# RetNet attention into a routed expert layer: scores in four quarters of the array, logits every second step, second keys turned in a scores' bank, and another order of the first loads

## The chip, the cores and the metric

The kernel runs on one core of a Trainium2 chip. The metric is the device time of one execution in microseconds. Five engines work side by side from queues of their own: TensorE (PE in the profile, PEld for its weight loads), VectorE (DVE), ScalarE (ACT), GpSimd (POOL) and SyncE (SP), which here issues nearly all DMAs.

## The reference

Two layers follow each other. The first is a recurrence over 768 positions for 4 batches of 8 heads of width 64; its result is the input of a layer of 8 experts, each row of 512 going to the expert with the highest logit.

```python
gamma = 1.0 - 2.0 ** (-5.0 - np.arange(H))
for t in range(S):                      # attention: q, k, v are (4, 8, 768, 64)
    state = gamma * state + k[:, :, t] (outer) v[:, :, t]
    y[:, :, t] = scale * q[:, :, t] @ state
x = y as rows of 8 heads x 64           # (3072, 512)
logits = x @ w_gate                     # (3072, 8)
e = argmax(logits); gate = softmax(logits)[e]
out = gate * (relu(x @ w1[e]) @ w2[e])  # w1 (8, 512, 1024), w2 (8, 1024, 512)
```

All data are float32.

## The kernel before

The attention runs in `STEPS = 12` steps, numbered 0 to 11. A step takes 128 positions of a pair of batches (`b` is 0 or 1) with all 8 heads, that is four pairs of heads `a`; `j` is the head within a pair, on partitions 0 to 63 or 64 to 127. The decay is folded into q and v: `scale_q` (GpSimd, for two steps at a time) and `scale_v` (GpSimd) write `qs` and `vs`. TensorE turns keys (`turn_k`, the tile `trk`, copied to `kT` by ScalarE) and queries (`turn_q`, `trq`, copied to `qT`), both one step ahead and inside the step before. In a step TensorE then does, in this order: `scores` (k times q, the tile `sc`, 64 rows by 128 columns of the array per product), `with_state` (q times the old state into `y`), `logits` of the step before (its `parts`), the turns of the next keys, `logits_of` (two transposes of the logits), in odd steps the turns of the next queries, `next_state` (the tile `new`), and `within` (masked scores times v, also into `y`). VectorE multiplies the scores with the causal mask (`am`), turns the finished `x` into rows (`to_rows`, the tile `xg`), reduces the logits (`lg`) and adds the state. ScalarE copies `x` out of PSUM.

Routing runs in pieces between the steps: `place(i)` is a generator, and `step(s, at)` pulls its next piece at a fixed place of a step (the table `WHEN`). `place(0)` covers steps 0 to 4 and begins in step 5, `place(1)` covers steps 5 to 8 and begins in step 9, `place(2)` covers the rest. `place(1)` ends with the row numbers `src_e` that GpSimd gathers for the early part of expert 0; after these gathers GpSimd writes one element of `w1t`, and only then may SP issue the first weights. In step 10 the second half of the masks (`am[1][1]()`) stands behind the routing's pieces. Step 11 ends in `early_rows`, and then the early expert layer begins (`hp`, `layer1`).

PSUM has eight banks: the tag `sc` has four (scores, `parts`, `trq`), `tr` two (`trk`, `new`, and the routing's `rk` and `found`), `y` two. Banks of a tag are taken in turn. Every engine's order is the order written in the program (`tc.manual_schedule`).

SP issues the DMAs in program order: a first list (lines 852 to 863), and then in step s the q, k and v of step s + 3 and the store of step s - 1 (`x_d<-xg`, four DMAs). `k` and `v` have 8 buffers, `q` 4, `xg` 3.

After the attention come the expert layers, one expert after the other (`p` at lines 233, 333, 246 and 474).

Of the kernel before, what the change touches and what calls it, by code (L numbers as in the profile page):

```python
# [21 lines left out]
P = 128  # L22
# [31 lines left out]
def kernel(  # L54
# [513 lines left out]
    with ExitStack() as actx:  # L568
# [19 lines left out]
        def load(nm, s, b, parts=1):  # L588
            m, b1, e = where[s]
            src = {"q": q, "k": k, "v": v}[nm]  # L590
            if nm == "q":
                to = att.tile([P, H, 2 * D], F32, tag=nm, name=nm, bufs=4)
                for part in (ts(i, H // parts) for i in range(parts)):
                    nc.sync.dma_start(to[:, part, :], src[2 * b1 + b, part, ts(m, 2 * P), :].rearrange(
                        "h (t e) d -> t h (e d)", e=2))
            else:
                to = att.tile([P, H, D], F32, tag=nm, name=nm, bufs=8)
                nc.sync.dma_start(to, src[2 * b1 + b, :, ts(2 * m + e, P), :].rearrange("h t d -> t h d"))  # L598
            raw[nm, s, b] = to
# [9 lines left out]
        def scale_v(s, b, by=nc.gpsimd):  # L609
            vs = att.tile([P, H, D], F32, tag="vs", name="vs", bufs=4)  # L610
            by.tensor_tensor(out=vs, in0=raw.pop(("v", s, b)), op=ALU.mult,  # L611
                             in1=inner(dec[:, ts(NC + 2 * where[s][0] + where[s][2], H)], D))
            raw["vs", s, b] = vs
# [5 lines left out]
        def pairs_of(tag, bufs, name):  # L619
            return ps(tag, bufs, name).rearrange("p (a t) -> p a t", a=HP)  # L620
# [10 lines left out]

        def turn_k(s, b):
            kT = att.tile([P, HP, P], F32, tag="kT", name="kT")
            tr = pairs_of("tr", 2, "trk")
            heads_first(raw["k", s, b], tr)
            nc.scalar.copy(out=kT, in_=tr)  # L636
            front[s, b] = kT
# [4 lines left out]
        def scores(s, b):  # L642
            kT, qT = front.pop((s, b)), q_of(s, b)
            sc = [pairs_of("sc", 4, "sc") for _ in range(2)]
            am = [att.tile([P, HP, P], F32, tag=f"am{j}", name=f"am{j}") for j in range(2)]
            for a in range(HP):
                for j in range(2):
                    r = ts(j, D)
                    nc.tensor.matmul(sc[j][:, a, :], lhsT=kT[r, a, :], rhs=qT[r, a, :], start=True, stop=True)  # L649

            def mask():
                for j in range(2):
                    nc.vector.tensor_tensor(out=am[j], in0=sc[j], in1=middle(causal[:, :], HP), op=ALU.mult)  # L653

            return am, mask
# [67 lines left out]

        early, wa = [], []

        def logits(s):
            bank = ps("sc", 4, "parts")
            parts = bank[:, 0 : 2 * P]
            m = P // DT
            for dt in range(DT):  # L730
                nc.tensor.matmul(parts[ts(dt, m), :], lhsT=wg[:, dt, :], start=True, stop=True,  # L731
                                 rhs=x[s][:, dt, :, :].rearrange("p b t -> p (b t)"))
            lgT = att.tile([P, 2 * P], F32, tag="lgT", name="lgT", bufs=1)
            nc.scalar.copy(out=lgT, in_=parts)
            return lgT, bank

        def logits_of(s, lgT, bank):
            tr = bank[:, 2 * P : 4 * P].rearrange("p (b t) -> p b t", b=2)
            for b in range(2):
                nc.tensor.transpose(tr[:, b, :], lgT[:, ts(b, P)], ident)  # L740
            return lambda: nc.vector.tensor_reduce(
                lg[:, 2 * s : 2 * s + 2, :], tr.rearrange("p b (a e) -> p b e a", a=DT)[:, :, 0:E, :], axis=AX.X,
                op=ALU.add)

        MOST_T = 2 * max(b - a for a, b in zip(NEXT, NEXT[1:]))

# [101 lines left out]
        def load_all(nm, s):  # L848
            for b in range(2):
                load(nm, s, b)  # L850
# [2 lines left out]
        load("k", 0, 0)  # L853
        load("q", 0, 1)
        load("k", 0, 1)
        nc.sync.dma_start(wg[:, :, 0:E], w_gate.rearrange("(dt p) e -> p dt e", p=P))
        load_all("v", 0)
        load_all("k", 1)
        load_all("v", 1)
        load("q", 2, 0)  # L860
        load("q", 2, 1)
        load_all("k", 2)
        load_all("v", 2)
        ctx.enter_context(tc.manual_schedule(engines={PE, ACT, POOL, DVE, SP}))
        xTa = first.tile([P, DT, EARLY], F32, tag="xTa", name="xTa")
# [32 lines left out]
        def step(s, at):  # L898
            for _ in range(WHEN.get(s, "").count(at)):
                next(rest, None)  # L900

        for s in range(STEPS):
            if s + 3 < STEPS:
                if s % 2:
                    load_all("q", s + 3)
                load_all("k", s + 3)
                if s == 7:
                    store(5)
                if s + 4 < STEPS:
                    load_all("v", s + 3)  # L910
            if s % 2 and s + 1 < STEPS:
                scale_q(s + 1, 1)
            if s + 2 < STEPS:
                for b in range(2):
                    scale_v(s + 1, b)
            if s % 2 == 0 and s + 2 < STEPS:
                scale_q(s + 2, 0)
            if s in (1, 2):
                nc.gpsimd.memset(xs2[s % 2], 0.0)
            if s:  # L920
                am = [scores(s, b) for b in range(2)]
                am[0][1]()
                step(s, "m")
                if s + 2 != STEPS:
                    am[1][1]()
            y = outputs()
            if s + 1 == STEPS:
                logit = logits(s - 1)
                rows_in_order()
            if where[s][0] or where[s][2]:  # L930
                with_state(s, y)

            def ahead():
                for b in range(2):
                    turn_k(s + 1, b)

            def ahead_q():
                if s % 2:
                    for b in range(2):
                        turn_q(s + 1, b)  # L940

            if s:
                if s + 1 < STEPS:
                    logit = logits(s - 1)
                    ahead()
                reduce = logits_of(s - 1, *logit)
                step(s, "p")
                if s + 2 == STEPS:
                    am[1][1]()
                    for b in range(2):  # L950
                        scale_v(s + 1, b)
                if s + 1 < STEPS:
                    ahead_q()
                to_rows(s - 1)
                reduce()
                if s == NEXT[NR - 1] + 1:
                    half_of_weights1(wa[0], 0, 0)
                if s != 6:
                    store(s - 1)
                if s + 1 == STEPS:  # L960
                    wa.append(weights2(first, 0, 2))
                if s == NEXT[NR - 1]:
                    load_all("v", STEPS - 1)
                if s == NEXT[NR - 1] + 1:
                    half_of_weights1(wa[0], 0, 1)
                if s in NEXT:
                    rest = chain(rest, place(NEXT.index(s) - 1))
                step(s, "a")
            next_state(s)
            step(s, "b")  # L970
            if s + 1 == STEPS:
                pad_ranks(acc[:, NR - 1, 0:2])
            step(s, "r")
            within(s, y, am, early_rows if s + 1 == STEPS else lambda: None)
            if s == 0:
                ahead()
            step(s, "c")

        egates, edst = gates_of(early[0], "_e"), targets(*early[:2], "_e")
# [6 lines left out]
        def within_early(f):  # L986
            nonlocal ne, arm, src, far
            if f == 1:
                logits_of(STEPS - 1, *logit)()
                next(rest)  # L990
                to_rows(STEPS - 1)
                store(STEPS - 1)
            if f == 2:
                gather(xs2[1], early[2][:, TC:], range(HALF), 2 * NEXT[NR - 1] * P)
            if f == 3:
                next(rest)
            if f == 4:
                ne = count()
                arm = arms(ne)
            if f == 5:  # L1000
                next(rest)
                next(rest, None)
                src, far = sources(inv, "")
                for e in range(2):
                    gather(xs2[e], src[:, ts(e, TC)], range(HALF, TC))
            if f > 5:
                which[f - 6] = regs(f - 6)
# [3 lines left out]
        for f in range(FT):  # L1011
            layer1(EARLY, xTa, wa[0], hTa, f, (("sc", 4),), lambda: within_early(f))
            if f == 0:
                logit = logits(STEPS - 1)
        hs = [att.tile([P, FH * P], F32, tag="k", name="he", bufs=8) for _ in range(4)]
        halves_of_w(wa[1], we, [0, 1])
        halves_of_h(hTa, hs, [0, 1])
# [279 lines left out]
```

## Time and profile before

| what | us |
|---|---|
| median of 3 runs | 439.13 |
| lowest and highest run | 437.85, 441.74 |
| the profiled execution | 442.87 |
| its span, first to last instruction | 441.2 |
| TensorE busy in the span | 420.9 |

The profiled execution is 1.67 us longer than its span, and 3.74 us longer than the median. A busy engine is one with an instruction in flight; the idle time in front of an instruction is put down to what released it, written with an arrow.

### The profile page before, as it was taken

How to read it: one execution, taken by the hardware profiler on the slowest of the kernel's cores; microseconds unless marked ns; L12 is line 12 of the kernel's file. 1: busy time of each engine (PE TensorE's matmuls, PEld its weight loads, DVE VectorE, ACT ScalarE, POOL GpSimd, SP SyncE). 2: the span in 40 equal slices, each digit the busy share in tenths (PEclk: the TensorE clock that was granted, in tenths of full speed). 3: DMA queues.
4: the chain of work that ended last, by engine and by line, in shares of the span. 5: the costliest groups of instructions: out<-in, count | busy, mean ns of one | idle time of the engine just before them, and what ended most of it. 6: DMA issues, size and time to landing. Idle time of an engine off the chain costs nothing.

```text
span 441.2 us, 9756 instructions
## 1 busy us (share of the span) xinstructions
PE 420.9 (95%) x3595; PEld 385.7 (87%) x3595; DVE 244.9 (56%) x565; ACT 130.4 (30%) x293; POOL 252.6 (57%) x212
## 2 busy tenths in 40 slices
PE   7889989999999999999999999999999999999990
PEld 4778877887788858999999999999999999999680
DVE  4445577769779960444672674377178247544320
ACT  2355452553521212201322222031223213303330
POOL 4477254553338352989329926983992892585051
PEclk9999999999999999999999999999999999999997
DMA  9989999999991497643955694496599449222222
GB/s 196 237 199 205 237 203 218 219 229 222 285 337 45 127 402 244 216 149 94 385 131 161 245 277 95 125 377 158 165 316 244 116 142 348 57 84 52 49 74 75
DMA packets 122123, 85.39 MB, mean 194 GB/s; under 512 B 56970, under 2 KB 106122, under 8 KB 122000
## 3 DMA queue, kind: packets, MB, share of 16 engines
q1 hardware_dynamic: 116736, 71.34, 59.5%
q0 software_dynamic: 5120, 12.60, 8.6%
q8 instruction: 49, 0.80, 0.8%
q14 instruction: 74, 0.61, 0.5%
q10 hardware_dynamic: 144, 0.05, 0.1%
HBM read 60.88 MB, written 14.68 MB: 171 GB/s over the span
## 4 chain that ended last, share of the span: by engine, by line
PE 82%; DMA 5%; SPq 4%; DVE 4%; issue 2%; ACT 1%; another core or an unknown queue 0%; POOLq 0%; DVEq 0%; ACTq 0%
PE p L333 51%; PE p L233 6%; DMA k<-in_k_dram 4%; PE p L246 4%; PE hp L233 3%; PE sc L649 3%; PE y L703 3%; SPq L598 3%; PE p L474 2%; PE new L685 2%; PE trq L617 2%; PE y L672 1%; PE trk L617 1%; DVE xTa L217 1%; PE parts L731 1%
## 5 line engine op out<-in xcount | busy, mean ns | idle before, releaser
L337 DVE TENSOR_TENSOR q<-p,q 128x196 f32<-128x196 f32 (+5 forms) x72 | 24.0, 352 | 41.8 <-PE p L333 35.1
L653 DVE TENSOR_TENSOR am<-sc,causal 128x512 f32<-128x512 f32 x48 | 30.0, 683 | 20.5 <-PE sc L649 20.4
L522 POOL DMA_INDIRECT out_dram<-o,dst x26 | 25.9, 996 | 26.4 <-ACT o L1167 19.5
L611 POOL TENSOR_TENSOR vs<-v,dec 128x512 f32<-128x512 f32 x23 | 24.6, 1084 | 26.5 <-DMA v<-in_v_dram 25.0
L174 POOL DMA_INDIRECT xs<-x_d,src x28 | 30.8, 1099 | 13.9 <-issue 9.8
L333 PE MATMUL p<-t,w1t 128*128 128x196 f32 (+5 forms) x192 | 35.9, 330 | 0.0
L333 PE MATMUL p<-t,s 128*128 128x196 f32 (+5 forms) x192 | 35.8, 329 | 0.0
L333 PE MATMUL p<-g,w2t 128*128 128x216 f32 (+5 forms) x192 | 35.3, 337 | 0.0
L337 DVE TENSOR_TENSOR yT<-p,q 128x216 f32<-128x216 f32 (+5 forms) x36 | 13.0, 374 | 39.5 <-PE p L333 31.0
L333 PE MATMUL p<-g,z 128*128 128x196 f32 (+4 forms) x192 | 33.6, 328 | 0.0
L333 PEld LDWEIGHTS p<-g,w2t 128*128 128x128 f32 x192 | 33.4, 190 | 0.0
L606 POOL TENSOR_TENSOR qs<-q,dec 128x512 f32<-128x512 f32 x22 | 22.4, 1044 | 19.1 <-DMA q<-in_q_dram 16.7
L337 DVE TENSOR_TENSOR hT<-p,q 128x196 f32<-128x196 f32 (+5 forms) x72 | 24.2, 351 | 16.0 <-PE p L333 15.6
L333 PE MATMUL p<-hT,w2t 128*128 128x196 f32 (+4 forms) x192 | 32.6, 328 | 0.0
L333 PEld LDWEIGHTS p<-t,w1t 128*128 128x128 f32 x192 | 32.4, 190 | 0.2 <-DVE q L337 0.2
L333 PEld LDWEIGHTS p<-t,s 128*128 128x128 f32 x192 | 32.5, 190 | 0.0
L1251 POOL COPY turn_of<-t 128x1 f32<-128x1 f32 x6 | 1.1, 184 | 54.5 <-DVE t L318 54.5
L333 PEld LDWEIGHTS p<-g,z 128*128 128x128 f32 x192 | 31.9, 190 | 0.0
L333 PEld LDWEIGHTS p<-hT,w2t 128*128 128x128 f32 x192 | 31.7, 190 | 0.0
L649 PE MATMUL sc<-qT,kT 64*128 64x128 f32 x384 | 24.9, 279 | 2.3 <-ACT kT L636 2.3
L649 PEld LDWEIGHTS sc<-qT,kT 64*128 64x128 f32 x384 | 22.4, 188 | 4.4 <-ACT kT L636 3.0
L703 PE MATMUL y<-am,vs 128*64 128x128 f32 x384 | 24.1, 274 | 0.5 <-issue 0.3
(231 smaller groups left out, 886.1 us busy)
## 6 DMA issues: line engine op xcount, KB each, us to landing
w1t<-in_moe_w_dram SPq DMA_DIRECT2D x7, 2048.0 KB
w2t<-in_moe_w_dram SPq DMA_DIRECT2D x7, 2048.0 KB
k<-in_k_dram SPq DMA_DIRECT2D x24, 256.0 KB
v<-in_v_dram SPq DMA_DIRECT2D x24, 256.0 KB
x_d<-xg SPq DMA_DIRECT2D x48, 128.0 KB
xs<-xs SPq DMA_DIRECT2D x96, 64.0 KB
o<-o SPq DMA_DIRECT2D x96, 64.0 KB
q<-in_q_dram SPq DMA_DIRECT2D x11, 512.0 KB
```

The costliest lines, as they stand in the source:

```text
L174: nc.gpsimd.indirect_dma_start(out=xs[:, t, :], out_offset=None, in_=x_d[0:rows, :], in_offset=bass.IndirectOffsetOnAxis(ap=idx[:, t : t + ...
L233: nc.tensor.matmul(hp, lhsT=w1t[:, 0, dt, ts(f, P)], rhs=xT[:, dt, n0:n], start=(dt == 0), stop=(dt == DT - 1))
L246: nc.tensor.matmul(y[j * z : j * z + m, 0:c], lhsT=hT[:, f, t * P + r0 : t * P + r0 + m], rhs=w2t[:, 0, f, ts(j, c)], start=(i == 0), stop ...
L333: nc.tensor.matmul(columns(y, c), lhsT=a, rhs=b, start=start and i == 0, stop=i + 1 == len(terms), skip_group_check=True)
L337: nc.vector.tensor_tensor(out=to, in0=y, in1=plus, op=ALU.add)
L522: done = nc.gpsimd.indirect_dma_start(out=out[:, :], out_offset=bass.IndirectOffsetOnAxis(ap=idx[:, t : t + 1], axis=0), in_=o[:, t, :], i ...
L606: by.tensor_tensor(out=qs[:, e, part, :], in0=got[:, part, ts(e, D)], op=ALU.mult, in1=inner(dec[:, ts(2 * where[s][0] + e, H)][:, part], D))
L611: by.tensor_tensor(out=vs, in0=raw.pop(("v", s, b)), op=ALU.mult, in1=inner(dec[:, ts(NC + 2 * where[s][0] + where[s][2], H)], D))
L617: nc.tensor.transpose(tr[:, a, :], src[:, 2 * a : 2 * a + 2, :].rearrange("p h d -> p (h d)"), ident)
L649: nc.tensor.matmul(sc[j][:, a, :], lhsT=kT[r, a, :], rhs=qT[r, a, :], start=True, stop=True)
L653: nc.vector.tensor_tensor(out=am[j], in0=sc[j], in1=middle(causal[:, :], HP), op=ALU.mult)
L703: nc.tensor.matmul(place_of(y, b, a, j), lhsT=vs[:, 2 * a + j, :], rhs=am[b][0][j][:, a, :], start=alone, stop=True, skip_group_check=True)
```

## The change

- `turn_k`: in even steps (the keys of odd steps), the second batch's keys are turned in a bank of the tag `sc` instead of `tr`.
- `scores`: each product of 64 rows by 128 columns of the array becomes two of 64 by 64, in two halves of the output's partitions; 16 products a step become 32.
- `logits` and `logits_of`: they take a list of steps. They run in odd steps only, for two steps at once (step 1: for step 0 alone; the last step of all alone, as before). Even steps have none. `lgT` is copied 512 wide, and four transposes go over the whole bank of `parts`.
- The first loads: the gate's weights `wg` go behind the second step's keys; `q` of step 2 and `k` of step 2 go before `v` of step 1.
- Step 0 scales both queries of step 2 before one `v` of step 1, the other `v` of step 1 is scaled on VectorE in step 1, and step 0 turns the keys of step 1 before `within` instead of after it.

```diff
 def turn_k(s, b):
-    tr = pairs_of("tr", 2, "trk")
+    tr = pairs_of("sc", 4, "trk") if s % 2 and b else pairs_of("tr", 2, "trk")
...
 def scores(s, b):
-                for j in range(2):
-                    r = ts(j, D)
-                    nc.tensor.matmul(sc[j][:, a, :], lhsT=kT[r, a, :], rhs=qT[r, a, :], start=True, stop=True)
+                for c in range(2):
+                    for j in range(2):
+                        r = ts(j, D)
+                        nc.tensor.matmul(sc[j][ts(c, D), a, :], lhsT=kT[r, a, ts(c, D)], rhs=qT[r, a, :],
+                                         start=True, stop=True)
...
-        def logits(s):
+        def logits(steps):
+            n = 2 * len(steps)
             bank = ps("sc", 4, "parts")
...
+            for i, s in enumerate(steps):
+                for dt in range(DT):
+                    nc.tensor.matmul(bank[ts(dt, m), ts(i, 2 * P)], lhsT=wg[:, dt, :], start=True, stop=True,
+                                     rhs=x[s][:, dt, :, :].rearrange("p b t -> p (b t)"))
+            lgT = att.tile([P, 4 * P], F32, tag="lgT", name="lgT", bufs=1)
+            nc.scalar.copy(out=lgT[:, 0 : n * P], in_=bank[:, 0 : n * P])
+            return steps, lgT, bank
+        def logits_of(steps, lgT, bank):
+            n = 2 * len(steps)
+            tr = bank[:, 0 : n * P].rearrange("p (b t) -> p b t", b=n)
+            for b in range(n):
                 nc.tensor.transpose(tr[:, b, :], lgT[:, ts(b, P)], ident)
...
-        nc.sync.dma_start(wg[:, :, 0:E], w_gate.rearrange("(dt p) e -> p dt e", p=P))
         load_all("v", 0)
         load_all("k", 1)
+        nc.sync.dma_start(wg[:, :, 0:E], w_gate.rearrange("(dt p) e -> p dt e", p=P))
+        load("q", 2, 0)
+        load_all("k", 2)
+        load("q", 2, 1)
         load_all("v", 1)
-        load("q", 2, 0)
-        load("q", 2, 1)
-        load_all("k", 2)
         load_all("v", 2)
...
-            if s % 2 and s + 1 < STEPS:
-                scale_q(s + 1, 1)
-            if s + 2 < STEPS:
+            if s == 0:
+                scale_q(2, 0)
+                scale_q(2, 1)
+                scale_v(1, 1)
+            elif s + 2 < STEPS:
+                if s % 2 and s > 1:
+                    scale_q(s + 1, 1)
                 for b in range(2):
                     scale_v(s + 1, b)
-            if s % 2 == 0 and s + 2 < STEPS:
-                scale_q(s + 2, 0)
+                if s % 2 == 0:
+                    scale_q(s + 2, 0)
...
             if s + 1 == STEPS:
-                logit = logits(s - 1)
+                logit = logits([s - 2, s - 1])
                 rows_in_order()
...
                 if s + 1 < STEPS:
-                    logit = logits(s - 1)
+                    if s % 2:
+                        logit = logits([s - 1] if s == 1 else [s - 2, s - 1])
                     ahead()
-                reduce = logits_of(s - 1, *logit)
+                reduce = logits_of(*logit) if s % 2 else lambda: None
...
                 reduce()
+                if s == 1:
+                    scale_v(1, 0, nc.vector)
...
             next_state(s)
+            if s == 0:
+                ahead()
             step(s, "b")
...
             within(s, y, am, early_rows if s + 1 == STEPS else lambda: None)
-            if s == 0:
-                ahead()
             step(s, "c")
```

## Rows read from the trace of the kernel before

**Rows 1.** The span cut into stages: start and end in us from the span's start, length, then busy us and instructions of TensorE, its weight loads, VectorE, ScalarE and GpSimd, the granted TensorE clock, the DMA engines' busy share, and GB/s.

```profile
24.06:59.20 35.14, 33.58 (x585) 29.17 (x585) 18.32 (x32) 17.12 (x33) 20.19 (x19) 1.00 0.98 213
59.20:78.62 19.42, 18.45 (x320) 15.48 (x320) 13.97 (x33) 8.94 (x18) 9.13 (x13) 1.00 0.95 216
78.62:97.02 18.40, 18.33 (x322) 16.10 (x323) 12.41 (x26) 8.49 (x17) 9.22 (x9) 1.00 1.01 219
97.02:111.65 14.63, 13.85 (x217) 11.52 (x215) 13.78 (x42) 7.04 (x14) 5.45 (x9) 1.00 0.94 217
111.65:118.72 7.07, 7.07 (x116) 5.74 (x115) 5.86 (x17) 3.75 (x7) 2.26 (x4) 1.00 0.93 283
147.95:441.20 293.25, 283.07 (x1688) 270.97 (x1688) 146.60 (x327) 71.32 (x180) 182.02 (x119) 0.99 0.59 184
```

**Rows 2.** SP's DMA issues in order of time: start, duration, line, what is moved, how many.

```profile
0.83 0.98 SPq L594 DMA_DIRECT2D q<-in_q_dram  x2
...
6.30 1.71 SPq L856 DMA_DIRECT2D wg<-in_moe_w_gate_dram  x1
...
86.81 4.39 SPq L598 DMA_DIRECT2D k<-in_k_dram  x2
91.30 3.53 SPq L721 DMA_DIRECT2D x_d<-xg  x4
...
106.52 1.10 SPq L598 DMA_DIRECT2D v<-in_v_dram  x2
111.95 0.37 SPq L158 DMA_DIRECT2D w1t<-in_moe_w_dram  x1
```

**Rows 3.** What TensorE waited for in the first 112 us: waiting line, releaser, us in total, times, longest.

```profile
PE trk L617 <- DMA k<-in_k_dram: 3.2, 6, 1.0
PE sc L649 <- ACT kT L636: 2.3, 3, 0.8
...
PE new L685 <- ACT kT L636: 0.5, 3, 0.2
```

**Rows 4.** TensorE in order of time, at the start and in steps 1, 3 and 4: start, duration, line, output and inputs, shape of the array, count, and in brackets the idle time before it.

```profile
1.54 4.21 PE L576 MATMUL warm<-idle 128*128 128x512 f32 x6 [1.54 <-DVE idle L574]
...
18.34 2.06 PE L649 MATMUL sc<-qT,kT 64*128 64x128 f32 x32 [0.85 <-ACT kT L636]
...
36.35 2.06 PE L649 MATMUL sc<-qT,kT 64*128 64x128 f32 x32
38.34 1.10 PE L672 MATMUL y<-qT,state 64*64 64x128 f32 x32
39.37 0.64 PE L731 MATMUL parts<-xT,wg 128*32 128x256 f32 x8
39.94 1.09 PE L617 MATMUL trk<-ident,k 128*128 128x128 f32 x8
...
50.27 0.38 PE L740 MATMUL parts<-ident,lgT 128*128 128x128 f32 x2
50.83 1.15 PE L685 MATMUL new<-vs,k 128*64 128x64 f32 x32 [0.17 <-ACT kT L636]
```

**Rows 5.** TensorE in order of time: the turns of keys in steps 5 and 7, and what follows in step 7.

```profile
58.26 0.66 PE L617 MATMUL trk<-ident,k 128*128 128x128 f32 x4 [0.94 <-DMA k<-in_k_dram]
59.20 0.66 PE L617 MATMUL trk<-ident,k 128*128 128x128 f32 x4 [0.28 <-DMA k<-in_k_dram]
...
78.62 0.66 PE L617 MATMUL trk<-ident,k 128*128 128x128 f32 x4 [0.39 <-DMA k<-in_k_dram]
79.11 0.38 PE L740 MATMUL parts<-ident,lgT 128*128 128x128 f32 x2
```

**Rows 6.** VectorE in order of time, steps 9 and 10.

```profile
97.02 1.31 DVE L714 STREAM_TRANSPOSE xg<-xT 128x512 f32<-128x512 f32 x2 [0.76 <-DMA x_d<-xg]
98.25 0.19 DVE L741 TENSOR_REDUCE lg<-parts 128x16 f32<-128x64 f32 x1
98.47 0.22 DVE L758 TENSOR_REDUCE mx<-lg 128x8 f32<-128x64 f32 x1
...
106.09 1.38 DVE L809 TENSOR_SCALAR here<-rrow,prow 128x128 bf16<-128x128 bf16 x8
107.81 0.32 DVE L829 TENSOR_TENSOR inv<-inv,found 128x160 f32<-128x160 f32 x1 [0.34 <-PE found L825]
...
108.86 1.28 DVE L653 TENSOR_TENSOR am<-sc,causal 128x512 f32<-128x512 f32 x2
```

**Rows 7.** TensorE in order of time, from the end of step 9 to the early expert layer, and the one wait behind it.

```profile
101.50 0.19 PE L783 MATMUL rk<-ohs,before 128*128 128x64 bf16 x1 [0.24 <-DVE ohs L765]
...
106.80 0.97 PE L825 MATMUL found<-val,here 128*128 128x160 bf16 x8
...
110.19 1.52 PE L703 MATMUL y<-am,vs 128*64 128x128 f32 x22 [0.17 <-DVE am L653]
111.65 2.06 PE L649 MATMUL sc<-qT,kT 64*128 64x128 f32 x32
113.68 0.64 PE L731 MATMUL parts<-xT,wg 128*32 128x256 f32 x8
...
118.72 1.99 PE L233 MATMUL hp<-xTa,w1t 128*128 128x256 f32 x8
...
147.95 7.36 PE L233 MATMUL p<-xTa,w1t 128*128 128x104 f32 x64 [0.33 <-DVE xTa L217]
```

More of the change, by code (lines that the diff above doesn't have):

```diff
@@ L724 @@
         early, wa = [], []
-        def logits(s):
+        def logits(steps):
+            n = 2 * len(steps)
             bank = ps("sc", 4, "parts")
-            parts = bank[:, 0 : 2 * P]
             m = P // DT
[L730 to L739, printed above, removed]
+            for i, s in enumerate(steps):
[9 more added lines that the diff above has]
+            for b in range(n):
                 nc.tensor.transpose(tr[:, b, :], lgT[:, ts(b, P)], ident)
             return lambda: nc.vector.tensor_reduce(
-                lg[:, 2 * s : 2 * s + 2, :], tr.rearrange("p b (a e) -> p b e a", a=DT)[:, :, 0:E, :], axis=AX.X,
-                op=ALU.add)
+                lg[:, 2 * steps[0] : 2 * steps[0] + n, :], tr.rearrange("p b (a e) -> p b e a", a=DT)[:, :, 0:E, :],
+                axis=AX.X, op=ALU.add)
         MOST_T = 2 * max(b - a for a, b in zip(NEXT, NEXT[1:]))
@@ L988, in within_early @@
             if f == 1:
-                logits_of(STEPS - 1, *logit)()
+                logits_of(*logit)()
                 next(rest)
@@ L1013 @@
             if f == 0:
-                logit = logits(STEPS - 1)
+                logit = logits([STEPS - 1])
         hs = [att.tile([P, FH * P], F32, tag="k", name="he", bufs=8) for _ in range(4)]
```

## Prediction

> **What bounds the kernel now.** I read the stages first. After 147.95 us TensorE is busy for 283.07 of 293.25 us and waits once for another engine, 0.33 us at its start [rows 1, 7]; nothing there is touched, so the whole effect is the shift of that start. Up to 111.65 us TensorE looks almost as full (18.33 of 18.40 us in one stage), but the DMA engines are at 0.94 to 1.01 of their time in the same stages, with some 215 GB/s [rows 1]. The reader is to see two nearly full resources and to ask which one the other waits for.
>
> SP's list answers. Each issue begins 0.04 to 0.10 us after the end of the one before, from 0.83 us to 107.62 (106.52 + 1.10): SP is never held by a buffer that the compute has not freed, it is held by the queue that it fills [rows 2]. So the landing times follow from the order of the loads and the DMA engines' rate, not from TensorE. TensorE meets that wall in steps 5 and 7: the keys come 0.94 and 0.28 us late at 58.26 and 59.20, and 0.39 us late at 78.62 [rows 5].
>
> The third meeting place is VectorE. In step 9 it waits 0.76 us, until 97.02, for a store of old rows (the buffer of `xg`), and the store stands in the same SP queue, at 91.30 to 94.83 [rows 2, 6]. From there VectorE is the chain: reduce, `place(1)`, masks, `here`; TensorE waits for it at 101.50 (0.24 us), `found` begins at 106.80 but cannot end before the last `here` (106.09 + 1.38 = 107.47), then `inv`, and the late masks from 108.86, for which the outputs at 110.19 wait [rows 6, 7]. In that stage VectorE is busy for 13.78 of 14.63 us [rows 1]. From 111.65 to 118.72 TensorE is full again, 7.07 of 7.07 us, and this is where a TensorE microsecond counts [rows 1].
>
> **The change part by part.**
>
> **Scores in quarters.** Now 32 records fill 1.99 us (36.35 to 38.34), and the next group, which already has the 64 by 64 shape, fills 1.03 us with 32 records (38.34 to 39.37) [rows 4]. At that price, 64 records would take 64 x 1.03/32 = 2.06 us, 0.07 more than now. The other bound takes away the entry into a new shape, which both groups have and which the two would now share. A stream of full 128-column transposes goes at 0.93/8 = 0.116 us (39.94 to 40.87, by the eight) [rows 4]; 24 groups of four at about that pace are 2.78 us for scores and state together, against 3.02 now: 0.24 less. I take 0.15 less a step, nearer the lower end because the second group pays its entry inside the 1.03. The Trainium skill (TensorEngine Tiling (Array Packing), Key Properties) says that a change of tiling mode drains TensorE; by it the common shape saves one drain a step, which is on the side I take (step 11 then grows by 0.65, without it by 0.87); no row isolates the drain.
>
> **Second keys in a scores' bank.** In even steps `new` waits for the first keys' copy. The two transposes before it start at 50.27 and need about 0.23 us, and `new` starts at 50.83: 0.33 us lost [rows 4]. With the second keys in a scores' bank `new` has its own, so the loss goes, in five even steps (in steps 8 and 10 `found` takes that place): up to 1.65 us. That bank must be free of its mask. The first batch's scores end some 1.0 us into the step and one mask lasts 0.64 (1.28 for two) [rows 6]; the second keys are turned 1.99 + 1.03 + 0.47 = 3.5 us into an even step, so there is no new wait.
>
> **Logits two at a time.** An even step loses its `parts` (39.37 to 39.94: 0.57 us) and its two transposes (0.23), an odd step has as much more: 0.8 us moved, none saved [rows 4]. One copy of 512 replaces two of 256 on ScalarE, off the path. The reduce on VectorE takes 0.19 us for 64 values and sits in the chain of step 9, where it now takes 128. Bounds: nothing, or a doubling (0.19). The next reduce, also of 64 values but to 8 results, takes 0.22 [rows 6], so most of such an instruction is fixed: I take 0.08.
>
> **First loads and first scaling.** The gate's weights keep SP for 1.71 us at 6.30 [rows 2]; they are moved, not dropped. The queue is the same sum up to the `v` of step 2. On TensorE, step 1 can gain the 0.85 us in which its scores wait for `kT` (its keys are now turned before `within`) [rows 4], and what its own keys cost: of 3.2 us of waits for k, 1.61 are the three of steps 5 and 7 shown, so at most 1.6 more [rows 3, 5]. Its price is that `v` of step 1 comes two loads later, behind `q`: the outputs of step 1 then wait. Together 0 to 2.4 us earlier at the start of step 2.
>
> **What is left at the end.** All that is gained before 58 us turns into a longer wait for the keys at 58.26 and 59.20. The same in step 7, at 78.62. Behind that TensorE carries 0.23 more in step 7 (four transposes for two), 0.8 + 0.33 + 0.15 less in step 8, 0.8 - 0.15 more in step 9: it reaches the routing's matmul at about 101.26 + 0.23 - 1.28 + 0.65 = 100.9, before VectorE is ready at 101.5. So VectorE's chain sets it: 101.50 + 0.08. In step 10 what TensorE no longer does (0.8 of logits, 0.33 of wait, 0.15 of scores) was cover for VectorE: `found` still ends with `here`. So the start of step 11 moves from 111.65 by +0.08. Step 11 now holds the logits of two steps, 0.8 more, and scores 0.15 less: the early layer starts 0.08 + 0.80 - 0.15 = 0.73 us later, at 119.45, and the shift goes through to the end.
>
> The profiled execution would be 442.87 + 0.73 = 443.6; it is one of the slower ones. On the median, 439.13 + 0.73 = **439.8 us**.
>
> **The rivals.**
>
> **The wall is soft.** If the keys and the store come as early as the faster TensorE frees buffers, the gains count: 2.4 at the start, 1.2 to 1.6 of waits in steps 5 and 7, 1.65 in even steps, 0.15 x 9, less 0.73: about 6 us, 433 us. Against it stands SP's list without a gap. For it: the DMA share stands for work in flight and the rate differs between stages. A part of this, 1 to 3 us, would come where the new order of loads changes the rate: 436.5 to 438.5.
>
> **Two at a time, the slower side.** In the changed order both products of one row half come two apart, with different column halves. If they cannot run together, the quarters run in pairs: 64 records at 1.99/32 = 0.062 us are 3.98 us, 1.99 more a step. Up to step 7 the wall hides most; from step 8 the chain of scores, masks and outputs takes it in steps 8 to 11, less the slack above: about 5 to 6 us, 445 us. The Trainium skill (TensorE: Matmul & The Clock Gate, Part 3, The mechanism) says that weights load beside running matmuls only where the row group differs, which is this rival. The rows speak against it: the state's products, four quarters with each row half twice, go at half the time per record of the scores [rows 4]. It decides where a quarter's weight load cannot pass the other column half.
>
> **The clock falls in a longer wait, also slower.** TensorE would stand still up to about 3 us before the keys of step 5, where its longest wait now is 1.0 [rows 3], at a granted clock of 1.00 throughout [rows 1]. At the start, after idling, the warm-up streams 2304 columns in 4.21 us, 1.83 ns each, against 0.97 in the early layer (2048 in 1.99) [rows 4, 7], about as 1.2 stands to 2.4 GHz. If such a stretch of 4 us came after step 7's wait, it would cost 2 us; the slack before 101.5 is 0.6: +1.4, 441.2 us.
>
> **It does not do what it says:** if `new` or the turned keys still wait in even steps, the time is that of the forecast, since those steps are in the wall's shadow.
>
> **How the numbers follow.** 0.60 for the forecast and the last rival, with its bounds from the reduce (0 to 0.19), the scores (-0.24 to +0.07) and the spread of a median: 438.8 to 441. 0.17 for a partly soft wall, 0.06 for a wholly soft one; 0.11 for the clock; 0.06 for two at a time. The range leaves out the wholly soft wall and the pairs: 436.5 to 442.5. Runs of this kernel spread from 437.85 to 441.74, so some 1% is what a measurement tells from no change; faster than 434.7 is 0.07, slower than 443.5 is 0.07, same 0.86.
>
> **What would show it.** Right: the keys of steps 6 and 8 still land near 59.2 and 78.6, with longer waits in front; `xg` of step 9 still begins near 97 after a store; the matmul `rk` of that step near 101.6; no idle time before `new` in even steps; scores and state together near 2.85 us; step 11 about 0.65 us longer, the early layer at 119.4. Wrong: the keys or that store land earlier by over 1 us; scores of 3 us and more; a granted clock under 1 between 55 and 80 us; or an early layer that starts before 118.7, which would say that VectorE's chain began earlier or that step 11 was not TensorE's.

## Result and the profile after

The changed kernel takes 441.06 us (median of 22 runs, 439.58 to 445.14), the kernel before beside it 439.09 (22 runs, 437.28 to 442.51): a ratio of 1.0051, 95% interval 1.0030 to 1.0073. The forecast was 439.8 against 439.13, that is +0.7; measured are +2.0, inside the range, on the forecast's side, and almost three times the size. It lies just above the 441 us up to which the prediction let its own mechanism reach. Timed again, it gave +2.1 in medians (ratio 1.0033, 1.0001 to 1.0064). Medians in this document are of all runs and ratios of the fast ones alone, which matters for the first loads alone below, where one execution of 626.37 us at a mean granted clock of 0.655 stands in the median and not in the ratio.

The profiled execution of after took 439.58 us, the fastest of its 22; that of before had taken 442.87, slower than any of the 22 timed beside after. The two traces are therefore no pair. A second trace of the kernel before (438.40 us, the last experiment) stands in for the first wherever times are compared here: it lies 1.2 us below the median of its runs, that of after 1.5 below.

The same stages in after, cut at its own events (columns as in [rows 1]):

```profile
23.02:58.29 35.27, 31.68 (x701) 27.38 (x700) 18.91 (x30) 16.21 (x30) 21.24 (x20) 1.00 0.95 215
58.29:77.12 18.83, 17.77 (x383) 15.31 (x383) 13.58 (x32) 8.79 (x17) 9.61 (x14) 1.00 0.99 230
77.12:94.88 17.76, 17.76 (x388) 16.18 (x389) 11.99 (x25) 8.48 (x16) 9.00 (x8) 1.00 1.01 224
94.88:109.26 14.38, 13.42 (x238) 11.03 (x237) 13.52 (x41) 6.61 (x13) 3.57 (x8) 1.00 0.93 209
109.26:117.36 8.10, 7.68 (x158) 6.09 (x158) 6.25 (x21) 4.43 (x8) 3.91 (x5) 1.00 0.80 243
146.56:437.87 291.31, 282.83 (x1688) 270.98 (x1688) 147.41 (x327) 72.38 (x180) 181.38 (x119) 0.99 0.59 186
```

TensorE is busy for less (31.68 of 35.27 us in the first stage, 33.58 of 35.14 in [rows 1]) and the DMA share up to step 10 is about as high as before (0.93 to 1.01, 0.94 to 1.01 in [rows 1]): what TensorE saved became idle time. The stage of step 11 grew from 7.07 to 8.10 us. What TensorE waits for in its first 112 us (columns as in [rows 3]):

```profile
PE trk L617 <- DMA k<-in_k_dram: 4.4, 5, 2.5
...
PE parts L734 <- issue: 0.5, 1, 0.5
```

The wait for keys grew from 3.2 to 4.4 us; `new` no longer waits for `kT`, but once, in step 1, 0.63 us for `vs` of GpSimd. In order of time (as in [rows 4, 5, 7]), steps 5 and 7, then the end of step 9 to the early layer:

```profile
50.97 1.98 PE L650 MATMUL sc<-qT,kT 64*64 64x128 f32 x64
52.77 1.05 PE L674 MATMUL y<-qT,state 64*64 64x128 f32 x32
53.75 1.07 PE L734 MATMUL parts<-xT,wg 128*32 128x256 f32 x16
57.27 0.66 PE L617 MATMUL trk<-ident,k 128*128 128x128 f32 x4 [2.46 <-DMA k<-in_k_dram]
58.29 0.66 PE L617 MATMUL trk<-ident,k 128*128 128x128 f32 x4 [0.36 <-DMA k<-in_k_dram]
...
75.23 0.63 PE L734 MATMUL parts<-xT,wg 128*32 128x256 f32 x5 [0.46 <-issue]
...
77.12 0.66 PE L617 MATMUL trk<-ident,k 128*128 128x128 f32 x4 [0.46 <-DMA k<-in_k_dram]
...
99.08 0.20 PE L787 MATMUL rk<-ohs,before 128*128 128x64 bf16 x1
...
109.26 1.98 PE L650 MATMUL sc<-qT,kT 64*64 64x128 f32 x64
111.17 1.07 PE L734 MATMUL parts<-xT,wg 128*32 128x256 f32 x16
...
117.36 1.97 PE L233 MATMUL hp<-xTa,w1t 128*128 128x256 f32 x8 [0.43 <-DMA w1t<-in_moe_w_dram]
```

Now the kernel before in its second trace, TensorE at the same places:

```profile
53.98 2.06 PE L649 MATMUL sc<-qT,kT 64*128 64x128 f32 x32
...
57.57 1.09 PE L617 MATMUL trk<-ident,k 128*128 128x128 f32 x8
...
76.19 0.66 PE L617 MATMUL trk<-ident,k 128*128 128x128 f32 x4 [0.23 <-DMA k<-in_k_dram]
...
98.76 0.20 PE L783 MATMUL rk<-ohs,before 128*128 128x64 bf16 x1
...
108.90 2.06 PE L649 MATMUL sc<-qT,kT 64*128 64x128 f32 x32
...
115.98 1.99 PE L233 MATMUL hp<-xTa,w1t 128*128 128x256 f32 x8
```

The step starts of the two (the first `sc` of each step, from the same views), in us:

| | step 2 | 5 | 6 | 7 | 8 | 9 | 10 | 11 | early layer |
|---|---|---|---|---|---|---|---|---|---|
| before, second trace | 29.23 | 53.98 | 63.81 | 71.71 | 81.57 | 90.15 | 99.10 | 108.90 | 115.98 |
| after | 28.04 | 50.97 | 64.31 | 70.94 | 82.72 | 90.05 | 99.41 | 109.26 | 117.36 |
| difference | -1.19 | -3.01 | +0.50 | -0.77 | +1.15 | -0.10 | +0.31 | +0.36 | +1.38 |

This table is the result in one line. TensorE is 3.01 us ahead at the start of step 5 and loses all of it and 0.50 more in that step: 2.82 in the two waits for its keys, most of the rest in the logits of a second step. It gains 1.27 in step 6 and loses 1.92 in step 7, gains 1.25 in step 8, loses 0.41 in step 9, and from there nothing is won back: step 11 costs 1.02 more, 0.43 of it a wait for `w1t`. From `p` to the end of the span the two executions differ by 0.19 us (291.50 and 291.31), so their spans, 436.7 and 437.9, differ by the front alone.

### The profile page after: what moved, and what is told of

Read it like the earlier page. It is cut to its first block, busy times and chain, and to the rows that moved or that the text cites. A ratio compares the mean times of both kernels' runs of the same rounds, so it can differ in the third digit from the quotient of the medians.

```text
span 437.9 us, 10497 instructions
## 1 busy us (share of the span) xinstructions
PE 418.2 (96%) x3979; PEld 384.5 (88%) x3979; DVE 245.5 (56%) x561; ACT 130.9 (30%) x288; POOL 250.1 (57%) x211
## 4 chain that ended last, share of the span: by engine, by line
PE 77%; DMA 11%; DVE 4%; SPq 3%; POOL 1%; issue 1%; POOLq 0%; ACT 0%; DVEq 0%
PE p L333 52%; PE p L233 7%; DMA k<-in_k_dram 4%; PE p L246 4%; PE hp L233 3%; PE p L474 3%; DMA q<-in_q_dram 3%; DMA v<-in_v_dram 2%; PE y L705 2%; PE sc L650 2%; PE new L687 1%; DVE xTa L217 1%; DMA w1t<-in_moe_w_dram 1%; PE trq L617 1%; PE trk L617 1%
## 5 line engine op out<-in xcount | busy, mean ns | idle before, releaser
L174 POOL DMA_INDIRECT xs<-x_d,src x28 | 29.5, 1054 | 14.8 <-issue 10.4
L611 POOL TENSOR_TENSOR vs<-v,dec 128x512 f32<-128x512 f32 x22 | 23.6, 1083 | 23.7 <-DMA v<-in_v_dram 16.8
L650 PE MATMUL sc<-qT,kT 64*64 64x128 f32 x768 | 24.0, 272 | 1.4 <-ACT kT L636 1.4
L380 ACT ACTIVATE hT<-p 128x196 f32<-128x196 f32 (+5 forms) x24 | 8.0, 334 | 55.1 <-PE p L333 55.1
```

The lines of the kernel that those rows point to most:

```text
L174: nc.gpsimd.indirect_dma_start(out=xs[:, t, :], out_offset=None, in_=x_d[0:rows, :], in_offset=bass.IndirectOffsetOnAxis(ap=idx[:, t : t + ...
L650: nc.tensor.matmul(sc[j][ts(c, D), a, :], lhsT=kT[r, a, ts(c, D)], rhs=qT[r, a, :], start=True, stop=True)
```

## Experiments

Every time is a median of executions, beside the kernel before on the same chip; ratios with 95% intervals. First the parts, each alone on the kernel before.

**The logits alone** (the changed `logits`, `logits_of` and their calls).

```diff
+                    if s % 2:
+                        logit = logits([s - 1] if s == 1 else [s - 2, s - 1])
```

> The kernel before with only the logits taken two steps at a time. Theory A (the forecast's: step 11 is TensorE's and now holds a second step's logits): 0.8 to 1.0 us slower than before, and the early layer starts that much later against the routing's gathers. Rival B (the new order of the first loads moves all later loads): no change here, within 0.4 us. Rival C (the quarters cost more somewhere than the rows say): no change here either.

440.88 against 440.29, ratio 1.0011 (0.9987 to 1.0034). TensorE in step 11:

```profile
111.72 2.06 PE L649 MATMUL sc<-qT,kT 64*128 64x128 f32 x32
113.70 1.07 PE L732 MATMUL parts<-xT,wg 128*32 128x256 f32 x16
...
119.40 0.92 PE L233 MATMUL hp<-xTa,w1t 128*128 128x256 f32 x3
```

Step 11 lasts 7.68 us, 0.61 more than the 7.07 of [rows 7] and the 7.08 of the second trace. The forecast's 0.80 for two steps' logits is 0.61; that step 11 pays for it is shown. In time it can't be told from no change, since the interval holds 1.

**The first loads alone** (the new list, the order of the scaling, and the turns ahead of `within` in step 0).

```diff
+        load("q", 2, 0)
+        load_all("k", 2)
+        load("q", 2, 1)
         load_all("v", 1)
```

> The kernel before with only the new order of the first loads, of the first scaling and of the first turns. Theory A: no change within 0.4 us, the gain at the start ends in the wait for keys in step 5. Rival B: 1.5 to 2 us slower, with the keys of steps 6 and 8 and the store in front of step 9's rows later by that much. Rival C: no change.

441.0 against 440.29, ratio 1.0003 (0.9979 to 1.0028): no change that can be told, and the 1.5 to 2 us of rival B (a ratio of 1.0034 and more) lie outside the interval.

**The quarters alone**, with the second keys in a scores' bank.

```diff
+                        nc.tensor.matmul(sc[j][ts(c, D), a, :], lhsT=kT[r, a, ts(c, D)], rhs=qT[r, a, :],
+                                         start=True, stop=True)
```

> The kernel before with only the scores in quarters and the second keys in a scores' bank. Theory A: 0 to 0.3 us faster, only step 11 and the stage behind it can show it. Rival B: the same. Rival C: 1 to 2 us slower.

441.15 against 440.29, ratio 1.0013 (0.9987 to 1.0040). Rival C's 1 to 2 us lie in good part inside this interval. No part alone can be told from the kernel before; the ratios add up to 1.0027, half of the whole's 1.0051, but with intervals of some 0.0025 to either side of each the sum may as well be the whole or nothing.

**Is it the loads that swallow the gain?** Both kernels without the loads of `v`: `k` is scaled in its place. The output is then another one and so is the routing, the same in both, so the pair is compared with itself and not with the rest.

```diff
+            if nm == "v":
+                return
...
-            by.tensor_tensor(out=vs, in0=raw.pop(("v", s, b)), op=ALU.mult,
+            by.tensor_tensor(out=vs, in0=raw["k", s, b], op=ALU.mult,
```

> The kernel before without the loads of v: k's tile is scaled in its place, so the output is not the reference's and 6.3 MB are not loaded. Wall theory: TensorE no longer waits for keys in steps 1, 5 and 7, VectorE not for the store in step 9, step 11 starts 3 to 6 us earlier than at 111.65. If the loads were no wall: step 11 within 1 us of 111.65.

> The changed kernel without the loads of v, with k's tile scaled in its place. Wall theory: what the change takes from TensorE now counts, so step 11 starts 2 us or more before that of the kernel before without v, and the whole is 1 us or more faster than that one, where with v it is 2 us slower. If the gains were lost for another reason: not faster than the kernel before without v.

Without `v`, the kernel before takes 444.16 (5 runs), the changed one 441.32 (10 runs): 2.8 us less, where with `v` it is 2.0 more. TensorE at the start of step 11 and of the early layer, first before without `v`, then after without `v`:

```profile
108.67 2.06 PE L651 MATMUL sc<-qT,kT 64*128 64x128 f32 x32
...
115.75 0.48 PE L233 MATMUL hp<-xTa,w1t 128*128 128x256 f32 x1
```

```profile
106.12 1.98 PE L652 MATMUL sc<-qT,kT 64*64 64x128 f32 x64
...
114.47 1.75 PE L233 MATMUL hp<-xTa,w1t 128*128 128x256 f32 x7 [0.68 <-DVE dst_e L203]
```

The step starts of the two, in us:

| | step 2 | 5 | 6 | 7 | 8 | 9 | 10 | 11 | early layer |
|---|---|---|---|---|---|---|---|---|---|
| before, without `v` | 27.56 | 51.77 | 61.60 | 69.50 | 78.90 | 90.03 | 98.85 | 108.67 | 115.75 |
| after, without `v` | 26.45 | 48.67 | 58.90 | 65.54 | 75.84 | 87.08 | 96.31 | 106.12 | 114.47 |
| difference | -1.11 | -3.10 | -2.70 | -3.96 | -3.06 | -2.95 | -2.54 | -2.55 | -1.28 |

With `v`, the lead of 3.01 us at step 5 was gone at step 6; without it, 2.70 of 3.10 are left there, and neither trace waits for keys in steps 5 and 7. With fewer bytes in the queue, step 11 begins 2.55 us earlier in the changed kernel, and even its longer step 11 leaves 1.28. So TensorE's savings are real, and it is the loads that take them away: shown. The size in time is less sure: against the kernel before with `v` the two have ratios of 1.0089 (1.0048 to 1.0131) and 1.0040 (1.0013 to 1.0066), which overlap, so the 1.5 us that the 2.8 has over the traces' 1.28 need no cause of their own.

The first expectation was just missed: step 11 begins 2.98 us before 111.65 instead of 3 to 6, and only 0.23 before the second trace with `v` (108.90). The pair has a limit of its own: on VectorE `here` of step 8 lasts 5.94 us in both (1.71 in after with `v`), and TensorE waits 2.48 and 2.13 us for masks.

**The changed kernel again, and step 11 with one step's logits.** In the second, steps 10 and 11 take one step's logits each, as before.

```diff
-                logit = logits([s - 2, s - 1])
+                logit = logits([s - 1])
...
-                    if s % 2:
+                    if s % 2 or s > 9:
```

> The changed kernel once more, unaltered, for a second trace beside the runs below. Theory D (the early layer waits for the first weights, whose landing the loads set, and TensorE's clock falls to half in some executions because it now waits longer in steps 5 and 7 and before the early layer): a mean granted clock of about 0.991 against 0.9935 of the kernel before, and in the trace a wait for w1t of 0.4 us or more. Theory A (only the logits of step 11): 0.7 us over before, the early layer without a wait for w1t, the clock as before.

> The changed kernel, but steps 10 and 11 take the logits of one step each, as before the change (two steps at once only up to step 9). Theory A: the 0.8 us of step 11 are gone, so 0.6 to 0.9 us faster than the changed kernel (measured 2.0 us slower than before), so about 1.2 us slower than before. Rivals B and C: as slow as the changed kernel, 2.0 us over before.

The repeat: 440.64 against 438.56, ratio 1.0033 (1.0001 to 1.0064). With single logits: 441.79 against 440.29, 1.0015 (0.9982 to 1.0047). Two things showed up that the forecast doesn't have. First the early layer waits for its weights, 1.64 us in the repeat, 2.44 in the other, here on TensorE:

```profile
119.88 2.78 PE L233 MATMUL hp<-xTa,w1t 128*128 128x256 f32 x8 [2.44 <-DMA w1t<-in_moe_w_dram]
```

Without that wait step 11 lasts 7.12 us there, 0.55 less than in after; the wait takes it back. Second, the granted clock falls to one half, 1.2 GHz. TensorE in the repeat, by stretches (length, busy, clock, DMA share, GB/s):

```profile
75.00:77.00 2.00, 1.51 (x6) 0.60 0.92 203
77.00:79.00 2.00, 2.00 (x12) 0.55 1.07 279
79.00:81.00 2.00, 2.00 (x33) 1.00 1.00 228
```

```profile
75.36 2.35 PE L617 MATMUL trk<-ident,k 128*128 128x128 f32 x8 [2.05 <-DMA k<-in_k_dram]
77.51 1.06 PE L744 MATMUL parts<-ident,lgT 128*128 128x128 f32 x4
```

After 2.05 us of waiting, the eight turns take 2.35 us instead of 1.09, the four transposes 1.06 instead of 0.60. The kernel with single logits has such a stretch in step 7 and another behind its wait for `w1t`, where `hp` to `p` lasts 30.77 us instead of 29.2. The first trace of after, with waits of 2.46 and 0.43 us, has none.

**The weights earlier.** GpSimd writes its element of `w1t` ahead of the two gathers, so that SP need not wait for these. In after they stand like this on GpSimd:

```profile
108.80 1.25 POOL L174 DMA_INDIRECT xs<-x_d,src_e  x1 [7.87 <-DMA v<-in_v_dram]
110.36 1.01 POOL L174 DMA_INDIRECT xs<-x_d,src_e  x1 [0.31 <-issue]
111.37 0.11 POOL L839 MEMSET w1t<- 128x1 f32 x1
```

They take their row numbers from `src_e`, which VectorE has written at 106.56:

```profile
106.39 0.17 DVE L188 TENSOR_SCALAR src_e<-tok_e 128x6 uint32<-128x6 f32 x1
```

The trace names a load of `v`, which these gathers don't read; they read the stored rows. They begin 2.24 us behind `src_e` and 3.1 us after SP's last issue of those stores ends (105.71), in the second trace of before 0.75 and 2.9 us (106.20 and 104.04; 106.95). That the stores' landing sets them fits these two and isn't shown. In the repeat and with single logits it is otherwise: the gathers begin 0.29 and 0.30 us behind `src_e`, 3.8 and 5.0 us after the stores' issue, so there VectorE's chain sets them.

```diff
-                gather(xs2[0], src[:, 0:TC], range(HALF), 2 * NEXT[i + 1] * P)
                 wa.append(first.tile([P, 1, DT, F], F32, tag="w1t", name="w1t"))
                 nc.gpsimd.memset(wa[0][:, 0, 0, 0:1], 0.0)
+                gather(xs2[0], src[:, 0:TC], range(HALF), 2 * NEXT[i + 1] * P)
```

> The changed kernel, with GpSimd's one-element write that frees the first weights' load placed before the two gathers instead of behind them. The load then goes out some 4 us earlier, at about 107 us. Theory D: the early layer no longer waits for w1t and starts right behind the last outputs of step 11, 0.4 to 2 us earlier, unless the gathers, which now share the DMA engines with 1 MB of weights, hold the rows back. Theory A: no change, TensorE reaches the early layer after the weights anyway.

The weights are issued at 105.69 instead of 111.51, step 11 begins at 110.45 and the early layer at 118.06, 7.61 later and without a wait. That step 11 is late has another cause in this trace: VectorE's `xg` of step 9 waits 2.61 us for a store, and TensorE's `rk` 1.08 us for VectorE. The time is 441.25 against 438.56, ratio 1.0053 (1.0031 to 1.0075). The wait goes in this trace, the 2 us stay: the landing of `w1t` alone isn't their cause.

**Keeping the clock up.** Idle matmuls (`warm`) stand in front of the keys of steps 5 and 7; the first version has four and two, and two more ahead of the early layer. The second has two and one, the third also has the single late logits.

```diff
             def ahead():
+                for _ in range({5: 2, 7: 1}.get(s, 0)):
+                    warm(512)
```

> The changed kernel with matmuls of 512 columns that nobody reads, in front of the turned keys in step 5 (four), step 7 (two) and in front of the early layer (two), so that TensorE does not stand still there. Theory D: the half-clock stretches are rarer, the mean granted clock goes back to about 0.9935, and the time comes 0.5 to 1 us below the changed kernel, though the two before the early layer may cost up to 0.9 us where the weights are early. Theory A: no gain, 0 to 0.9 us slower than the changed kernel, the clock unchanged.

> The changed kernel with three matmuls of 512 columns that nobody reads, two before the turned keys in step 5 and one in step 7 (some 0.85 us each), so that TensorE stands still for less of the wait there. Theory D (the change costs 0.7 us in step 11, and in some executions a fall of the clock after a longer wait for keys): the falls are rare, the mean granted clock near 0.994 and the median 1 to 1.5 us under the changed kernel, about 0.7 over before. Rival E (the clock is a by-product, the time is lost elsewhere): clock back, but the median as the changed kernel or up to 1 us above.

> The same three matmuls, and steps 10 and 11 with the logits of one step each. Theory D: both costs are gone, the median within 0.5 us of the kernel before. Rival E: 1 us and more over before.

The first took 446.46 (ratio 1.0172, 1.0145 to 1.0200) and says little: an idle matmul of 512 columns lasts about 0.9 us, twice what I had allowed for, and the fill was longer than the waits. The second, TensorE in step 5 and at the end:

```profile
55.17 1.98 PE L576 MATMUL warm<-idle 128*128 128x512 f32 x4
56.99 1.38 PE L617 MATMUL trk<-ident,k 128*128 128x128 f32 x8
...
109.53 1.98 PE L650 MATMUL sc<-qT,kT 64*64 64x128 f32 x64
...
117.13 1.99 PE L233 MATMUL hp<-xTa,w1t 128*128 128x256 f32 x8
```

Here the idle work fits the waits (steps 6 and 8 begin at 63.73 and 82.57, in after at 64.31 and 82.72), the mean clock of the runs is 0.994 as in the kernel before (0.993; the changed kernel 0.991), and the time is 442.37 against 440.14, ratio 1.0043 (1.0023 to 1.0063). The third: 442.43, 1.0057 (1.0033 to 1.0082); its step 11 lasts 7.04 us (109.94 to 116.98), 0.56 less than the second's 7.60, and the median doesn't show it. A clock that is as high as before doesn't bring the time back. That clock falls cost nothing isn't shown by it: in the repeat, runs with a lower mean clock are longer (correlation -0.8), in the first 22 runs less so (-0.3).

**The kernel before, a second time.**

> The kernel before, unchanged, timed against itself. Every theory expects a ratio of 1.000 with an interval that holds 1; if it comes out beyond 1.002 on either side, differences of 0.6 to 0.9 us between the parts say nothing. Its trace is the second look at the kernel before, whose first profiled execution was 442.9 us, one of its slowest. Theory wall (the time in front of the early layer is set by loads and stores and by step 11): the early layer begins within 0.5 us of 118.72, and xg of step 9 at 97.0. Rival (the first execution was slow in front of the early layer): it begins at 117.5 or earlier, and the change then costs more there than the first pair of traces shows. Third possibility: the two traces of one kernel differ by 1 us and more behind 148 us or at the very end, and then the 2 us of the change cannot be placed with single traces.

439.59 against 439.90, ratio 1.000 (0.9979 to 1.0022). Its early layer begins at 115.98, not 118.72: 2.74 us between two executions of one kernel, which is more than the change is worth. The expectation's rival holds, and the third possibility too (`p` to the last `yT`: 283.1 us and 284.8). Of these 1.7 us TensorE's products make 0.25: from `p` to the start of its last group are 280.94 us here and 281.19 in the first trace. The rest lies behind them, where the last `yT` begins 2.16 us after the start of that group here and 3.63 in the first trace. There it waits for something that the profile only calls `remote`. First the second trace, then the first:

```profile
428.30 0.48 DVE L480 SCALAR_TENSOR_TENSOR yT<-p,gate,q 128x256 f32<-128x256 f32 x1 [1.47 <-PE p L474]
```

```profile
432.77 0.48 DVE L480 SCALAR_TENSOR_TENSOR yT<-p,gate,q 128x256 f32<-128x256 f32 x1 [2.95 <-remote]
```

VectorE in step 9, in the second trace of before:

```profile
94.38 1.31 DVE L714 STREAM_TRANSPOSE xg<-xT 128x512 f32<-128x512 f32 x2 [0.56 <-ACT lgT L734]
95.61 0.19 DVE L741 TENSOR_REDUCE lg<-parts 128x16 f32<-128x64 f32 x1
```

and in after:

```profile
94.88 1.30 DVE L716 STREAM_TRANSPOSE xg<-xT 128x512 f32<-128x512 f32 x2 [1.19 <-DMA x_d<-xg]
96.11 0.25 DVE L745 TENSOR_REDUCE lg<-parts 128x32 f32<-128x128 f32 x1
```

In this execution of the kernel before, `xg` waits for ScalarE's copy of TensorE's logits and not for a store; `rk` at 98.76 waits for nobody. There TensorE itself leads from step 8 to the start of step 10. In the first trace the store came at least 2.6 us later (97.02), and TensorE seemed to have time to spare. Such a wait of `rk` for VectorE, behind a late store, stands in other traces too: 0.69 us with the logits alone, 0.62 with the first loads alone, 1.08 with the early weights.

## Why the prediction came out as it did

**Right.** The loads swallow what TensorE gains before steps 5 and 7: the keys are turned at 57.27 and 58.29 behind a wait of 2.46 and 0.36 us ([rows 5] has 0.94 and 0.28), and the pair without `v` shows that it is the loads. The gain itself is as estimated: 1.19 at step 2 (of 0 to 2.4), 3.01 by step 5. In even steps `new` doesn't wait any more, and step 8 is 1.25 us shorter, against the 1.28 of the sum. Its up to 1.65 us for five such waits were too many, though: [rows 3] has three. Scores and state take 53.75 - 50.97 = 2.78 us, the lower bound (3.02 before), so 0.24 a step instead of 0.15. Step 10 doesn't get shorter: it lasts 9.79 to 9.85 us in every trace of these experiments, whatever TensorE saves in it, and its last outputs wait for VectorE's masks. SP's list is again without a gap over 0.13 us up to the first weights, but for one of 0.52 before the stores at 64.31.

Step 11 gets longer by 0.59 without its wait, against 0.65, partly by luck: its second step of logits costs 0.61 (the logits alone) instead of 0.80, and there `parts` stands between scores and state, so that the two don't follow each other in one shape and the scores give 0.12 (111.17 - 109.26 = 1.91 us, 2.03 in [rows 7]).

**The rivals.** Two at a time is refuted: 64 records of quarters fill 1.80 us (50.97 to 52.77), 0.028 each, not 0.062. The Trainium skill (TensorE: Matmul & The Clock Gate, Part 3, The mechanism) would have weights load beside running products only where the row group differs; here the two products of one row half, with different column halves, come two apart without that price. The Trainium skill (TensorEngine Tiling (Array Packing), Key Properties) has a change of mode drain the array; two groups that now share one shape are 0.24 us shorter, which agrees, though no run separates the drain from the rest.

A soft wall is refuted by the pair with and without `v`: with `v` the lead is gone at step 6. The prediction's sign for it, keys or store over 1 us earlier, did appear against the first trace (77.12 for 78.62, `xg` at 94.88 for 97.02), but the second trace of the same kernel is earlier still (76.19, 94.38): the times that these signs were read from were those of a late execution. The clock's fall does occur in some executions, and with it that rival's loss: in the repeat the turns and transposes of the half-clock stretch take 1.72 us more, where the rival had 2. "It does not do what it says" is refuted by `new`.

**The slack in step 9 was not one of the kernel.** "it reaches the routing's matmul at about 101.26 + 0.23 - 1.28 + 0.65 = 100.9, before VectorE is ready at 101.5. So VectorE's chain sets it": the 0.6 us of slack were read from an execution 3.7 us above the median, whose loads and stores came some 2.5 us late. Its own time stood beside the median in the text, but the place of the difference was not looked for; most of it lay in front of the early layer, in the very waits from which the slack was read. In the second trace TensorE reaches `rk` without a wait.

The loss doesn't come from this, however. Without the slack the prediction's own terms (+0.23 - 1.28 + 0.65) would begin step 11 by 0.40 us earlier, not later. In the pair of traces it begins 0.36 later because the last keys of step 7 are turned 0.93 later (77.12 for 76.19); behind them come +0.22 in step 7, -1.25 in step 8, +0.41 in step 9 and +0.05 in step 10. Whether the change or the execution made these keys late isn't shown: the two traces of before differ by 2.43 there (78.62 and 76.19).

**Wrong: nothing was late for the early layer.** The forecast lets it begin when TensorE is done, at 0.08 + 0.80 - 0.15 = 0.73, and has no term for the landing of `w1t`. The weights were late by 0.43 and 1.64 us in the two traces of the changed kernel, and by 2.44 with single logits; in neither trace of before does TensorE wait for them. A later issue isn't the reason in the two longer waits: there `w1t` was issued at 110.05 and 110.63, before the 111.51 of the first trace of after, and the early layer began 9.02 and 9.25 us behind the issue, in after 5.85. Why the transfer takes longer in some executions stays open, and so does what the change has to do with it.

For the one good pair of traces the sum is then +0.36 at step 11 (forecast +0.08), +0.59 in it (forecast +0.65), +0.43 for the weights (no term): +1.38 in front, +1.2 in the span, against a forecast of +0.73.

**Open.** From +1.2 to the +2.0 of the medians there remain 0.8 us, the ratio's interval allows 0.1 to 2.0. Longer waits for `w1t` and falls of the clock would fill it in some executions (the repeat's trace begins its early layer at 119.07, the earlier one at 117.36). But the kernels that remove one of the two, the early weights and the small fill, stayed at +2.7 and +2.2. Either each alone suffices, or something is at work that no trace here isolates; a kernel with both wasn't tried. Single traces can't settle it: from `p` to the last `yT` they take 282.9 to 286.5 us, where all these kernels do the same work, and the kernel before alone has 284.8 and 283.1. So of the 2.0 us some 0.6 are shown, in step 11; the rest is not placed.

## What to carry to other kernels

Before a slack of half a microsecond is read from a profile, compare the profiled execution with the median, and if it is slower by more than the slack, find where it lost that: a wait that stands there in a late execution need not stand in an ordinary one. Savings ahead of a queue that is full, as the loads are here up to step 7, only turn into waits; work that is moved into the last steps before the queue runs dry is then paid in full. Look at every transfer that the next stage needs, and at what must land before it may be issued.

## What was not expected of the hardware

- The granted clock fell to one half behind a wait for keys of 2.05 us in the repeat (step 7) and of 2.03 with the early weights (step 5, 0.50 from 58 to 60 us), and not behind one of 2.46 in the first trace of after.
- TensorE stood still for 0.46 us in the middle of `parts` in step 7 of after, with no releaser (`issue`), for 1.2 in the repeat and 2.2 in sum with the small fill and single logits. The changed kernel has 980 records in its first 55 us instead of 736, but that isn't needed for it: kernels with the old scores stand still too, 0.40 us among the products with the state with the first loads alone, 0.49 in `parts` with the logits alone, and in the second trace of before the products with the state in step 3 last 1.65 us instead of 1.10. Here the wait of step 7 lay in front of keys that were late anyway.
- Two executions of one kernel, with the same products in the same order, differ by 1.7 us from `p` to the last `yT`, and TensorE has a part of 0.25 in it.
